# First half of the third pair's values in the visit of its state update, a VectorE read in place of the drain

## Chip, cores, metric

One core of one Trainium2 chip. The time of a run is the device time of the whole program in microseconds. Each engine works through an instruction queue of its own: TensorE (PE, with weight loads as a row of their own, PEld), VectorE (DVE), ScalarE (ACT), GpSimd (POOL) and SyncE (SP), which issues most DMAs.

## What is computed

Block-wise linear attention with decay over 4 batches of 8 heads (768 positions, head size 64), and then, on its output of 3072 tokens by 512, a feed-forward layer with the gate h·cos(h):

```python
for b in range(nb):                       # blocks of 64 positions
    intra = einsum('bhic,bhjc->bhij', qb, kb) * Dmask
    intra = einsum('bhij,bhjd->bhid', intra, vb)
    inter = einsum('bhid,bhde->bhie', qb * lam_pow, kv_state)
    out[:, :, sl] = intra + inter
    kv_state = lam_block * kv_state + einsum('bhsd,bhse->bhde', kb * rev_pow, vb)
# then, with x the attention's output as 3072 x 512
h = x @ w_in                              # 512 x 2048
out = (h * cos(h)) @ w_out                # 2048 x 512
```

## The kernel before

The tokens are cut into 24 blocks of 128, taken in 12 pairs. A pair's two blocks (s = 0, 1) come from two batches. Pairs 0 and 1 (the "spans") are computed in a way of their own at the start. Pairs 2 to 11 run the general code; pair 2 (blocks 4 and 5) is the third pair, and the first of these. The feed-forward layer runs over tiles of blocks (TILES: 4, 2, 2, 2, 2, 2, 2, 4, 4), and pair 2 is the attention for tile 1, done while tile 0's projections run.

A pair's attention on TensorE has these tasks, all of 64-by-64 tiles, four of which fill the array:

- *scores* (L416 to L423): k by q for each half of 64 positions of each block, 32 matmuls into two PSUM banks ps_s; VectorE multiplies by the mask into s_m (L425 to L427).
- *update* (L429 to L435): k by v for the state, 32 matmuls into the banks ps_kv; VectorE adds it to the running sum or writes the state S (L437 to L442), ScalarE casts the sums to S (L444). For pair 2 ("early") VectorE writes the first half's S straight away, and the sums later.
- *values* (L488 to L497): s_m by v, the halves (s=1, half 0) and (s=0, half 1), 16 matmuls into two banks ps_o.
- *values_carried* (L503 to L518): the halves (0, 0) and (1, 1) of the values, 16 matmuls, and then q by S, 32 matmuls (16 where no state is carried in), which add up in the same banks.

The first half of the values writes the banks with other row halves of the array than the second, and has the matmuls that start the accumulation; the second half must not overtake it. The program has three ways for this. Where the next pair's scores and update stand between the halves ("more", pairs 6 to 10), VectorE reads one element of ps_o after the first half ("turn", L499 to L501) and the second half waits for that read. Where the pair is in APART (3, 4, 5, 11), the first half goes to banks of its own, ps_x. For pair 2, which is neither, the queue is drained between the halves (L504, L505).

Nothing is scheduled by hand: a Planner (L56 to L140) gets every task with its engine, a duration, what it depends on, a priority and how many of the eight PSUM banks it takes, and simulates the engines. It takes, at each step, the task that can start first, by priority among equals; a task with `then` set lets only that other task follow on its engine. The order of the planned starts is the order of the instructions in each engine's queue, DMA issues on SP among them. The durations are the program's own estimates (QUART 0.0317 for a group of four small matmuls, SW 0.11 for a change of tile shape), and bear on the order alone.

Around the change the order is: tile 0's projections (L784) in groups of four, three groups for each of four blocks and then each block's last group. The update of pair 2 comes after block 1's last group, values and values_carried together after block 2's, and block 3's last group is held behind values_carried (`closing.deps.append(v12[SPANS])`, L858). Then tile 1's hidden matmuls (L738) begin, which need pair 2's output xT (L520 to L525, copied by VectorE for s = 0 and ScalarE for s = 1). The lines that join scores and update to the plan are L447 to L471; for the early pair the update isn't tied to the scores.

Of the kernel before, what the change touches and what calls it, by code (L numbers as in the profile page):

```python
# [18 lines left out]
SPANS = 2  # L19
# [124 lines left out]
def kernel(  # L144
# [38 lines left out]
    def bank(i, shape, dt, name):  # L183
        return psum.tile(shape, dt, tag=f"bank{i}", bufs=1, name=name)
# [57 lines left out]
    pl = Planner({**BUFS, "q_f": BUFS["ld"], "k_f": BUFS["ld"], "v_f": BUFS["ld"]})  # L242
    MM = lambda cols, n=1: n * (cols / 2400.0 + 0.0025)

    SW = 0.11
# [6 lines left out]
    def prio_attn(n, part):  # L252
        i = next(i for i in range(len(TILES)) if n < first[i + 1])
        return begins[i - 1] + unit[i - 1] * (n - n % 2 - first[i] + 2 * part) / TILES[i]
# [68 lines left out]
    T, So, Vo, d_t, Uo, Uo_sp = ({} for _ in range(6))  # L323
    qkT_head, qk_head, v_head, v12 = {}, {}, {}, {}
    chunks = [(halves[c], c) for c in range(2)]

    def tile_of(n):
        return next((i, n - first[i]) for i in range(len(TILES)) if n < first[i + 1])
# [69 lines left out]
    QUART = 0.0317  # L398
# [71 lines left out]
        qk_head[pr].frees = [T[pr, 0], T[pr, 1], u]  # L470
        return s_t, u  # L471

    def add_stretch(pr):

        n0 = 2 * pr
        g, c = divmod(pr, NB)
        pa = lambda part: prio_attn(n0, part)
        tile_i, j0 = tile_of(n0)

        def value(s, half, o=None):  # L480
            m = halves[half]
            o = live["o", n0 + s][:, :, m] if o is None else o
            for h in range(H):
                yield lambda h=h: nc.tensor.matmul(  # L484
                    o[halves[h % 2], h // 2], lhsT=live["v_s", n0 + s][m, h, :], rhs=live["s_m", n0 + s][m, h, :],
                    start=(apart or s != half) and h < 2, stop=True, skip_group_check=True)

        def values(t):  # L488
            for s in range(2):
                live["o", n0 + s] = bank(t.bank[s], [P, NP, P], F32, "ps_o")  # L490
            cross = [None, None]
            if apart:

                cross = live["cross", pr] = [bank(i, [P, NP, D], F32, "ps_x") for i in t.bank[2:]]
            for x, y in zip(value(1, 0, cross[0]), value(0, 1, cross[1])):
                x()
                y()  # L497

        def turn(_):  # L499

            live["turn", pr] = nc.vector.tensor_copy(spare[D:D + 1, 0:1], live["o", n0][D:D + 1, NP - 1, D:D + 1])  # L501

        def values_carried(_):  # L503
            if not more and not apart:  # L504
                nc.tensor.drain()  # L505
            for x, y in zip(value(0, 0), value(1, 1)):
                i = x()
                y()
                if ("turn", pr) in live:
                    tc.add_manual_dep(i.ins, live.pop(("turn", pr)).ins.name, mybir.DependencyInfo(  # L510
                        mybir.DependencyClass.Sync, mybir.DependencyReason.DATA), reason="row halves in turn")
            for half in range(0 if c else 1, 2):
                S = live["S", pr, 0] if half else live["S", pr - 1, 1]
                for h in range(H):
                    for s, r in enumerate(halves):
                        nc.tensor.matmul(live["o", n0 + s][halves[h % 2], h // 2, halves[half]], lhsT=S[r, h, :],  # L516
                                         rhs=live["qkT", pr][r, 0, h, halves[half]],
                                         start=False, stop=True, skip_group_check=True)  # L518

        def values_out(_, s, e):  # L520
            if ("xT", tile_i) not in live:
                live["xT", tile_i] = work.tile([P, KD, 4 * P], BF16, tag="xT", name="xT")
            j = j0 + s
            (nc.vector.tensor_copy if e == "DVE" else nc.scalar.copy)(  # L524
                live["xT", tile_i][:, :, j * P:(j + 1) * P], live.pop(("o", n0 + s)))  # L525

        def halves_out(_, s, half):
            if ("xT", tile_i) not in live:
                live["xT", tile_i] = work.tile([P, KD, 4 * P], BF16, tag="xT", name="xT")
            o, i = live["o", n0 + s][:, :, halves[half]], (j0 + s) * P + half * D  # L530
            x = live["xT", tile_i][:, :, i:i + D]
            if s == half:
                nc.scalar.copy(x, o)
            elif half or c:
                nc.vector.tensor_add(x, o, live["cross_f", pr][half])  # L535
            else:
                nc.vector.tensor_copy(x, live["cross_f", pr][half])

        def cross_out(_, half):
            live.setdefault(("cross_f", pr), {})[half] = toks.tile([P, NP, D], F32, tag=f"cross{half}", bufs=1, name=f"cross{half}")  # L540
            nc.scalar.copy(live["cross_f", pr][half], live["cross", pr][half])

        deps = [So[n0], So[n0 + 1], Uo[pr, 0], Uo.get((pr - 1, 1)) if c else None]
        more = pr + 1 < NBLK // 2 and pr + 1 not in ALONE
        apart = pr in APART
        v1 = pl.add("PE", 4 * QUART + SW, deps, values, pa(0.5), banks=2 + 2 * apart)
        chain = [v1]
        if more:
            nxt = list(add_scores(pr + 1, pa(0.5)))
            for t in nxt:  # L550
                v1.deps += [d for d in t.deps if d not in nxt]
            chain += nxt
        if more:
            deps = deps + [pl.add("DVE", 0.12, [v1], turn, pa(-9.0))]
        v2 = v12[pr] = pl.add("PE", (12 if c else 8) * QUART + (0.0 if more or apart else 0.28), deps, values_carried, pa(0.5))
        chain.append(v2)
        v1.bank_frees = []
        if apart:
            after = [v2] + ([h_last[tile_i - 2]] if tile_i >= 2 else [])
            copies = [pl.add("ACT", 0.42, after, partial(halves_out, s=s, half=s), pa(0.6)) for s in range(2)]  # L560
            moved = [pl.add("ACT", 0.42, [v1], partial(cross_out, half=half), pa(0.55)) for half in range(2)]
            sums = [pl.add("DVE", 0.4, after + [moved[1 - s]], partial(halves_out, s=s, half=1 - s), pa(0.0 if pr == SPANS else 0.59 - 0.01 * s)) for s in range(2)]
            for s in range(2):
                Vo[n0 + s] = [copies[s], sums[s]]
            v1.bank_frees = [Vo[n0], Vo[n0 + 1], [moved[0]], [moved[1]]]
        for s in range(2):
            So[n0 + s].frees = [v2]
            v_head[n0 + s].frees = [v2]
            if apart:
                continue  # L570
            e = "DVE" if pr == SPANS and s == 0 else "ACT"
            Vo[n0 + s] = [pl.add(e, 0.65, [v2] + ([h_last[tile_i - 2]] if tile_i >= 2 else []), partial(values_out, s=s, e=e),
                                 pa(0.0 if e == "DVE" else 0.6))]
            v1.bank_frees.append(Vo[n0 + s])
        qkT_head[pr].frees = [v2]
        if (pr + 1, 1) in Uo:
            Uo[pr + 1, 1].deps.append(v2)
        for x, y in zip(chain, chain[1:]):
            x.then = y
            y.deps.append(x)  # L580
# [242 lines left out]
    for at, name in enumerate(names):  # L823
        which, n = name[0], int(name[1:])
        soft = which in "io"
        deps = [kept[-3 if soft else -2]] if at and (names[at - 1][0] in "io") != soft else []
        if name == f"q{2 * SPANS}":
            deps = []
        if name == f"v{2 * SPANS}":
            deps = [load_t["k_f", 2 * SPANS]]  # L830
        if name == "o3":
            deps = [load_t["q_f", 2 * SPANS]]
# [10 lines left out]
    add_span_state()  # L843
    for pr in range(SPANS, NBLK // 2):
        prepare(pr)
    add_scores(SPANS, prio_attn(2 * SPANS, 0.2))
    pr = SPANS
    for i in range(len(TILES)):
        while 2 * pr < first[i + 1]:
            if pr + 1 in ALONE:  # L850
                add_scores(pr + 1, prio_attn(2 * pr + 2, 0.2))
            add_stretch(pr)
            pr += 1
        add_ffn(i)
    for f in range(2, SPLIT):
# [60 lines left out]
```

## Time and profile before

| | us |
|---|---|
| median of 4 runs (204.35, 205.24, 204.19, 205.19) | 204.77 |
| the profiled execution, its time | 204.35 |
| its span in the profile | 202.6 |
| PE busy | 194.9 (96%) |
| ACT, DVE, POOL busy | 120.0, 116.6, 64.8 |
| PE hidden L738 and projections L784, busy | 90.5 and 88.3 |

TensorE's granted clock is at 9 tenths or more in every slice (0.999 in the mean). The profile's chain of waits goes back from the last instruction to what released each; a line gives the start, the length and the group of instructions. "issue" is time in which the engine waited for nothing that the profile shows. Other views are groups by source line (shortest, median and longest duration in ns), and the timeline, in which a row merges instructions of one line that follow each other.

VectorE around the change, from the timeline (start, length, group, idle time before it and what ended it):

```profile
42.73 0.77 DVE L352 TENSOR_TENSOR v_s<-v_f,v_scale 128x512 bf16<-128x512 f32 x1 [0.51 <-DMA v_f<-in_v_dram]
44.80 0.69 DVE L440 TENSOR_TENSOR S<-sum,ps_kv 128x512 bf16<-128x512 f32 x1 [1.30 <-PE ps_kv L434]
46.81 0.69 DVE L524 CAST xT<-ps_o 128x512 bf16<-128x512 f32 x1 [1.32 <-PE ps_o L516]
47.42 1.40 DVE L440 TENSOR_TENSOR sum<-sum,ps_kv 128x512 f32<-128x512 f32 x2
```

### The profile page before, as it was taken

The numbers are of one execution on the slowest core, as the hardware profiler recorded it, in microseconds if no ns is written. First come the engines' busy times: TensorE is split into PE (matmuls) and PEld (weight loads), VectorE is DVE, ScalarE is ACT, GpSimd is POOL, SyncE is SP. The second block draws the span as 40 slices with busy tenths as digits, with TensorE's granted clock in tenths as the row PEclk, the third lists the DMA queues.
The fourth block names the chain that finished last, engine by engine and source line by source line (L and its number), as shares of the span: only waits on it lengthen the run. The fifth ranks groups of instructions, "written<-read, shape, count | busy, mean of one in ns | idle before, by whom it ended". The sixth has DMA issues, their size and how long they took to land.

```text
span 202.6 us, 5913 instructions
## 1 busy us (share of the span) xinstructions
PE 194.9 (96%) x2441; PEld 116.9 (58%) x2469; DVE 116.6 (58%) x228; ACT 120.0 (59%) x240; POOL 64.8 (32%) x85
## 2 busy tenths in 40 slices
PE   6999999999999999999999999999999999999994
PEld 2567444547847848666658676755445444444443
DVE  2878774256954967848548575734579544444001
ACT  5978872128937868565639676653877655355120
POOL 5694004056144462726255373543500000000000
PEclk9999999999999999999999999999999999999999
DMA  4999999999999998999899999979900010111112
GB/s 119 320 192 203 204 203 219 176 224 252 211 248 170 282 212 208 227 173 273 166 259 213 212 187 263 203 186 260 209 0 3 3 52 0 52 55 52 52 52 104
DMA packets 96762, 33.94 MB, mean 167 GB/s; under 512 B 84320, under 2 KB 93792, under 8 KB 96736
## 3 DMA queue, kind: packets, MB, share of 16 engines
q1 hardware_dynamic: 89232, 28.78, 64.1%
q0 software_dynamic: 7360, 4.72, 16.2%
q8 instruction: 19, 0.31, 0.6%
q10 hardware_dynamic: 144, 0.07, 0.1%
q14 instruction: 7, 0.06, 0.1%
HBM read 27.27 MB, written 6.29 MB: 166 GB/s over the span
## 4 chain that ended last, share of the span: by engine, by line
PE 92%; DMA 3%; issue 2%; SPq 2%; POOL 1%; ACT 0%; POOLq 0%; ACTq 0%
PE ps_h L738 41%; PE ps_f L784 40%; DMA sp_f<-in_k_dram 3%; PE ps_o L484 2%; PE ps_s L422 2%; PE ps_kv L434 2%; PE ps_o L516 2%; SPq L268 1%; PE ps_o L644 1%; PE ps_kv L631 1%; POOL k_sp L599 1%; PE ps_x L484 0%; PE ps_t L374 0%; PE ps_t L607 0%; PE ps_kv L705 0%
## 5 line engine op out<-in xcount | busy, mean ns | idle before, releaser
L750 DVE TENSOR_TENSOR g<-ps_h,cos 128x256 bf16<-128x256 f32 (+1 forms) x148 | 73.2, 504 | 42.8 <-ACT cos L744 41.9
L744 ACT ACTIVATE cos<-ps_h,halfpi 128x256 f32<-128x256 f32 (+1 forms) x148 | 75.7, 539 | 29.4 <-PE ps_h L738 28.5
L738 PE MATMUL ps_h<-xT,w_in_sb 128*128 128x256 bf16 (+1 forms) x586 | 90.5, 304 | 0.5 <-issue 0.3
L784 PE MATMUL ps_f<-w_out_sb,g 128*128 128x512 bf16 (+2 forms) x378 | 88.3, 370 | 2.0 <-issue 1.3
L738 PEld LDWEIGHTS <-w_in_sb 128*128 128x128 bf16 x592 | 57.1, 98 | 30.2 <-DVE xT L524 0.4
L784 PEld LDWEIGHTS <-g 128*128 128x128 bf16 x400 | 37.6, 98 | 37.2
L344 POOL TENSOR_TENSOR qk<-q_f,q_scale 128x512 bf16<-128x512 f32 x19 | 19.7, 1044 | 38.0 <-DMA q_f<-in_q_dram 29.2
L798 ACT COPY o_sb<-ps_f 128x512 f32<-128x512 f32 (+1 forms) x24 | 13.8, 573 | 30.0 <-PE ps_f L784 29.9
L352 POOL TENSOR_TENSOR v_s<-v_f,v_scale 128x512 bf16<-128x512 f32 x19 | 19.7, 1044 | 15.8 <-DMA v_f<-in_v_dram 13.0
L427 DVE TENSOR_TENSOR s_m<-ps_s,mask 128x512 bf16<-128x512 f32 x20 | 13.0, 685 | 3.6 <-PE ps_s L422 3.0
L348 POOL CAST qk<-k_f 128x512 bf16<-128x512 f32 x18 | 11.0, 613 | 8.0 <-DMA k_f<-in_k_dram 7.8
L524 ACT CAST xT<-ps_o 128x512 bf16<-128x512 f32 x11 | 6.0, 589 | 9.7 <-PE ps_o L516 6.4
L440 DVE TENSOR_TENSOR sum<-sum,ps_kv 128x512 f32<-128x512 f32 x15 | 10.2, 682 | 0.6
L445 ACT CAST S<-sum 128x512 bf16<-128x512 f32 x15 | 9.2, 618 | 0.9 <-DVE sum L440 0.8
L798 DVE COPY o_sb<-ps_f 128x384 f32<-128x384 f32 x1 | 0.6, 558 | 11.5 <-DMA out_dram<-o_sb 11.5
L876 PE MATMUL ps_idle<-blank 128*128 128x512 f32 (+2 forms) x8 | 5.4, 824 | 1.6 <-DVE blank L211 1.6
L484 PEld LDWEIGHTS <-v_s 64*64 64x64 bf16 x320 | 3.9, 107 | 4.1 <-issue 3.6
L623 DVE TENSOR_TENSOR s_m_sp<-ps_s,mask_sp 128x512 bf16<-128x512 f32 x8 | 5.1, 684 | 1.1 <-PE ps_s L618 1.1
L484 PE MATMUL ps_o<-s_m,v_s 64*64 64x64 bf16 x256 | 5.1, 197 | 0.1
L712 POOL CAST S<-sum 128x512 bf16<-128x512 f32 x1 | 0.6, 607 | 14.0 <-DVE sum L709 14.0
L501 DVE COPY spare<-ps_o 1x1 f32<-1x1 f32 x5 | 0.8, 156 | 7.3 <-PE ps_o L484 7.3
L535 DVE TENSOR_TENSOR xT<-ps_o,cross 128x256 bf16<-128x256 f32 x8 | 3.1, 421 | 3.0 <-PE ps_o L516 2.0
(74 smaller groups left out, 96.1 us busy)
## 6 DMA issues: line engine op xcount, KB each, us to landing
q_f<-in_q_dram SPq DMA_DIRECT2D x20, 256.0 KB, 3.7
k_f<-in_k_dram SPq DMA_DIRECT2D x20, 256.0 KB, 4.1
v_f<-in_v_dram SPq DMA_DIRECT2D x20, 256.0 KB, 4.5
out_dram<-o_sb SPq DMA_DIRECT2D x19, 256.0 KB, 2.4
w_out_sb<-in_moe_w_out_dram POOLq DMA_DIRECT2D x4, 512.0 KB, 12.2
sp_f<-in_q_dram SPq DMA_DIRECT2D x2, 512.0 KB, 5.2
sp_f<-in_k_dram SPq DMA_DIRECT2D x2, 512.0 KB, 5.7
w_in_sb<-in_moe_w_in_dram POOLq DMA_DIRECT2D x4, 256.0 KB, 6.9
```

Of the source, the lines that this page charges most:

```text
L344: vec[e].tensor_mul(new_qk()[:, 0, :, s], live.pop(("q_f", 2 * pr + s)), q_scale[:, c, :].unsqueeze(2).to_broadcast([P, H, D]))
L348: (nc.scalar.copy if early else nc.gpsimd.tensor_copy)(new_qk()[:, 1, :, s], live.pop(("k_f", 2 * pr + s)))
L352: vec[e].tensor_mul(live["v_s", 2 * pr + s], live.pop(("v_f", 2 * pr + s)), v_scale[:, c, :].unsqueeze(2).to_broadcast([P, H, D]))
L427: nc.vector.tensor_mul(t, live["s", pr][s], mask.unsqueeze(1).to_broadcast([P, H, D]))
L440: nc.vector.tensor_add(new, live["sum", pr, 0] if half else live["sum", pr - 1, 1], live["kv", pr][half])
L445: nc.scalar.copy(new_S(pr, half), live["sum", pr, half])
L484: yield lambda h=h: nc.tensor.matmul(o[halves[h % 2], h // 2], lhsT=live["v_s", n0 + s][m, h, :], rhs=live["s_m", n0 + s][m, h, :], start= ...
L738: nc.tensor.matmul(t[:, :n], lhsT=w_in_sb[:, kd, f * P:(f + 1) * P], rhs=live["xT", i][:, kd, at], start=(kd == 0), stop=(kd == KD - 1))
L744: nc.scalar.activation(c[:, :n], live["h", i, f, at.start][:, :n], AF.Sin, bias=halfpi)
L750: return nc.vector.tensor_mul(live["g", i][:, f, at], live.pop(("h", i, f, at.start))[:, :n], live.pop(("c", i, f, at.start))[:, :n])
L784: nc.tensor.matmul(live["f", i, j, piece][:, :width], lhsT=live["g", i][:, f, j * P:(j + 1) * P], rhs=w_out_sb[:, f, part], start=(f == 0) ...
L798: (nc.scalar.copy if eng == "ACT" else nc.vector.tensor_copy)(o[:, :width], live["f", i, j, piece][:, :width])
```

## The change

For pair 2 alone, `add_stretch` gets the pair's update task as `ahead`. The task *values* takes over the update's dependencies and priority beside those on s_m, holds its two banks from then on, and is tied to the update, which follows it at once. *values_carried* loses the drain, and waits for the VectorE read "turn" of ps_o, as in the pairs 6 to 10. In the planner's figures for it, the 0.28 of the drain is replaced by one SW.

```diff
-    def add_stretch(pr):
+    def add_stretch(pr, ahead=None):
...
         def values_carried(_):
-            if not more and not apart:
+            if not more and not apart and not ahead:
                 nc.tensor.drain()
...
-        v1 = pl.add("PE", 4 * QUART + SW, deps, values, pa(0.5), banks=2 + 2 * apart)
-        chain = [v1]
+        if ahead:
+            v1 = pl.add("PE", 4 * QUART + SW, [So[n0], So[n0 + 1]] + ahead.deps, values, ahead.prio, banks=2)
+            v1.then = ahead
+            ahead.deps.append(v1)
+            chain = []
+        else:
+            v1 = pl.add("PE", 4 * QUART + SW, deps, values, pa(0.5), banks=2 + 2 * apart)
+            chain = [v1]
...
-        if more:
+        if more or ahead:
             deps = deps + [pl.add("DVE", 0.12, [v1], turn, pa(-9.0))]
-        v2 = v12[pr] = pl.add("PE", (12 if c else 8) * QUART + (0.0 if more or apart else 0.28), deps, values_carried, pa(0.5))
+        v2 = v12[pr] = pl.add("PE", (12 if c else 8) * QUART + (SW if ahead else 0.0), deps, values_carried, pa(0.5))
...
-    add_scores(SPANS, prio_attn(2 * SPANS, 0.2))
+    first_scores, first_update = add_scores(SPANS, prio_attn(2 * SPANS, 0.2))
...
-            add_stretch(pr)
+            add_stretch(pr, first_update if pr == SPANS else None)
```

## The prediction

> **What bounds the kernel now.** I read the page first for what sets the end, then the chain of waits around the change, then the timeline there for what each wait hangs on.
>
> ```profile
> span 202.6 us, 5913 instructions
> PE 194.9 (96%) x2441; PEld 116.9 (58%) x2469; DVE 116.6 (58%) x228; ACT 120.0 (59%) x240; POOL 64.8 (32%) x85
> PE 92%; DMA 3%; issue 2%; SPq 2%; POOL 1%; ACT 0%; POOLq 0%; ACTq 0%
> ```
>
> TensorE carries 92% of the chain that ends last; the other engines are near 60% or below. So the end moves by whatever TensorE's queue gets shorter or longer, as long as nothing new makes it wait. The chain where the third pair (pair 2, blocks 4 and 5) is done:
>
> ```profile
> 40.97 3.40 PE ps_f L784 x15
> 44.37 0.38 PE ps_kv L434 x32
> 44.74 0.54 PE ps_f L784 x2
> 45.28 0.05 issue
> 45.33 0.38 PE ps_f L784
> 45.71 0.25 PE ps_o L484 x16
> 45.96 0.10 issue
> 46.06 0.32 PE ps_o L484 x16
> 46.38 0.28 PE ps_o L516 x32
> 46.66 0.16 issue
> 46.82 0.81 PE ps_f L784 x3
> ```
>
> Columns: start, length, what. The pair comes twice: the update at 44.37, and after one group of four projections (L784) the values at 45.71, both without a break in TensorE's row. Between the two halves of the values stand 0.10 us of nothing, and then a second half of 0.32 us. That is the drain: as an instruction of its own it has a record
>
> ```profile
> L505 PEldq DRAIN  x1: 338/338/338, 45.7 to 45.7; - x1
> ```
>
> (338 ns in the weight loads' queue, partly beside the first half's matmuls). It is the only one in the program: pair 2 alone is neither followed in its visit by the next pair's scores nor among APART.
>
> For what a visit costs without a drain there are two kinds of rows, the APART visit of pair 3 and the visit of pair 6, which waits for the VectorE read instead:
>
> ```profile
> 60.67 0.25 PE ps_x L484 x16
> 60.92 0.13 PE ps_o L484 x16
> 61.05 0.34 PE ps_o L516 x32
> 104.51 0.25 PE ps_o L484 x16
> 104.76 0.26 PE ps_s L422 x32
> 105.02 0.32 PE ps_kv L434 x32
> 105.34 0.16 PE ps_o L484 x16
> ```
>
> The first small group of a visit takes 0.25 us for 16 matmuls, later ones 0.13 to 0.16 for 16 and 0.26 to 0.35 for 32. Whoever comes first in a visit pays about 0.1 us for the change from 128-wide to 64-wide tiles; every visit also ends on 0.16 us of "issue".
>
> **The change, part by part.**
>
> 1. Update visit. It takes 44.74 − 44.37 = 0.37 us. Afterwards the moved half comes first, at 0.25 (the row of any first half), and the 32 update matmuls come behind a group of the same tile shape: 0.29 at 56.82 and 70.15, where they follow scores, 0.32 at 105.02. Sum 0.54 to 0.57, so **+0.17 to +0.20**.
>
> 2. Values visit. It takes 46.82 − 45.71 = 1.11 us with its closing issue. Afterwards: the second half now comes first, 0.25; the 32 carried matmuls 0.28 (here) to 0.35; the issue of 0.16. Sum 0.69 to 0.76, so **−0.35 to −0.42**.
>
> 3. Together **−0.15 to −0.25 us; I take −0.20**. It is nearly the drain alone, for the moved half goes into a visit that is there anyway and pays no tile change of its own. A check the other way: the second half with the drain's gap, 0.10 + 0.32, against 0.16 at 105.34 gives −0.26, the upper end. The Trainium skill ("TensorE: Matmul & The Clock Gate", Single matmul latency) puts a matmul that can't hide its pipe at (398 + N)/2.4 ns when warm, 193 ns for N = 64; the rows' small matmuls are 193 ns each in the middle. A drain would then cost 193 ns less one spacing (0.13/16 = 8 ns), estimated at 0.185 us, and the sum would be −0.185 by the rule against up to −0.26 by the row. I stay with the visits' own rows.
>
> 4. The VectorE read ("turn", L501). Five rows of this form take 156 ns, and start 0.05 to 0.06 us after the first half's end (104.76 to 104.82, 116.88 to 116.93). Here the half ends at about 44.37 + 0.25 = 44.62, so the read stands at 44.68 to 44.84. VectorE's row is empty there: its v_s product ends at 43.50 and the state S starts at 44.80, 0.06 after the update's end. In the new order the update ends at 44.91 to 44.94 and S can't start before 44.97, 0.13 after the read is gone. So the read costs S nothing. If that cover were gone, S would come up to 0.16 later.
>
> 5. The wait for the read. Behind it on TensorE stand the second half, the carried matmuls, block 3's last projections and then tile 1's hidden matmuls; ScalarE's and VectorE's xT copies wait for the carried ones. The visit can't come before the four projections are through, 44.92 + 0.97 = 45.89; the read has been done for 1.05 us by then. Nothing.
>
> 6. S. Before: 44.80 to 45.49, the visit at 45.71, 0.22 of slack. After: 44.98 to 45.67 against 45.89, the same 0.22, and 0.25 more since only the carried matmuls behind the second half read S. Nothing.
>
> 7. The moved half's own waits. It wants both s_m tiles (VectorE, L427, 40.93 + 1.29 = 42.22) and the v_s tiles for which the update waits already (42.95 and 43.50). TensorE gets there at 44.3. Nothing; if the v_s products came 0.9 us later, old and new order would both wait.
>
> 8. PSUM banks. Now 2 banks of ps_o are held from 44.3, beside 2 of ps_kv. The four projections of tile 0 hold 4 at most: blocks 0 and 1 are copied out at 43.54 and 44.40, 2 and 3 at 45.75 and 47.66 (L798). 4 + 4 is exactly 8, and the last of the other four to come free are the scores' banks, at 42.22. It fits with 2 us to spare, but there is no ninth bank.
>
> 9. Semaphores. The Trainium skill ("Perfetto Trace Analysis", Identifying Dependency Chains) warns that an instruction that waits for several engines may get an EventSemaphore instruction put ahead of it, which speaks against joining two tasks with different producers. The trace has such a row at the update of the later visits:
>
> ```profile
> L434 PEldq EVENT_SEMAPHORE  x8: 51/51/51, 56.5 to 152.8; - x8
> ```
>
> Added in both visits at full price, it would take the sum to −0.20 + 2 × 0.05 = −0.10. But the visit at 56.38 has one and its update still takes 0.29: it lies beside matmuls. I count nothing and keep 0.10 for the range.
>
> 10. What it issues and passes: no DMA. Block 2's output copy (45.75) and its store come 0.18 us later, block 3's (47.66) 0.20 earlier; both buffers have time, since the SP queue sends them among loads.
>
> 11. What comes after. From 47.6 on TensorE's row has no wait but the 0.16s and the tile changes; all of it moves up 0.20 us, if the planner keeps its order. Its own figures for the pair shrink by 0.17 (0.28 for the drain goes, 0.11 for a second switch comes), so a visit could slip only where its data are due within 0.17 of the place it has now. In the plan of before, the visits that hang on a DMA have 0.33 us or more; those that hang on S move with the rest. I expect the same order.
>
> Against the profiled execution: 204.35 − 0.20 = 204.15 us, span 202.4. The median of the runs is 204.77, 0.42 above that execution, so **204.57 us**, −0.1%. The four runs lie at 204.19 to 205.24; a difference below 0.5% (1.02 us) is not told from none, and the forecast is "no change" in that sense.
>
> **Rivals.**
>
> *The gain is eaten* (0.10): both event semaphores are paid, or the read does fall in front of S, +0.10 to +0.16, and the moved half costs the upper end. Sum about 0.0, 204.77. For it: the 0.13 between the read's end and S is thin. Against: five rows in which the read lies clear of its neighbours.
>
> *The pair is put off by its banks* (0.16): slower. Place: the update. Two tasks are tied together that need four banks while the four projections hold four. If the planner, with its own times, finds one not free, the tied pair goes behind block 2's projections. Then nothing lies between the update and the carried matmuls: block 3's end waits for the values by the program's own rule, tile 1 for xT. TensorE waits 0.06 + 0.69 (S) + up to 0.16 (the read) + about 0.1 = 0.9 to 1.0 us, less the gain: +0.75. It decides as soon as the scores' banks come free later than block 1's group ends, 2 us from now. If later value visits then slip a group behind too, each loses what the 1.67 us of projections after it (61.55, 74.45, 105.81) no longer cover: the xT copies end at 62.4 and hidden starts at 63.06, so a slip of 0.86 costs 0.2. Two of these: +1.2, 205.97. Against: step 8.
>
> *A better order by luck* (0.10): the shift of 0.17 joins visits downstream or takes tile changes away. A visit's entry (0.1), the wait for the last projection (0.38 against 0.22) and its exit (0.16) are about 0.42; to lose 1.02 in all, two such visits would have to merge: 204.57 − 0.84 = 203.7. Nothing in the profile asks for it. That the change doesn't do what it says is no case of weight: the drain has a single record.
>
> *The forecast* has 0.64.
>
> **Numbers.** Forecast and eaten gain both lie within 0.5%: 0.74 less a little for scatter, 0.72. Slower is the bank rival and scatter, 0.16; faster is the lucky order and scatter, 0.12. Range: bounds of the forecast (−0.25 to 0.0 on 204.77) and the scatter of the runs (about 0.5 either side) give 204.0 to 205.3; a part of each outer case takes it to 203.8 and 205.5.
>
> **What would show it.** No DRAIN record; L501 six times, the first near 44.7; the update visit with 16 ps_o and 32 ps_kv at 0.54 to 0.57; S starting 0.06 after the update, not after the read; the values visit at 0.69 to 0.76; the first hidden matmul of tile 1 0.2 us earlier, and the same distance at the end. Wrong would be: an idle stretch before the update or the carried matmuls, a wait on the read, visits at other places after 50 us.

## The result, and the profile after

| | before | after |
|---|---|---|
| median, us | 204.24 (54 runs) | 203.92 (33 runs) |
| ratio | | 0.9979, 95% interval 0.9973 to 0.9985 |
| the same again, beside later experiments | 204.24 (34 runs) | 203.96 (14 runs), ratio 0.9986 (0.9971 to 1.0001) |
| span of the profiled execution | 202.6 | 202.2 |

The change takes about 0.3 us off: clear of noise in the first interval (that of the later runs just reaches 1), within the half per cent that the forecast called "no change", and somewhat more than the 0.20 that was forecast. The four runs that the prediction had (median 204.77) held two from the thin upper end of this program's runs: 10 of the 54 lie at 204.7 or above. So the forecast of 204.57 was built on a base 0.53 too high; its difference is what to judge. That 203.92 still lies inside the forecast range, 0.12 above its lower end, is owed to the width of the range.

The page after, busy time of TensorE, in which the share of the span is as before:

```profile
span 202.2 us, 5913 instructions
PE 193.8 (96%) x2441; PEld 116.4 (58%) x2469; DVE 116.7 (58%) x229; ACT 120.0 (59%) x240; POOL 64.8 (32%) x85
```

The chain of waits at pair 2 after the change (start, length, what; L485, L517, L745 and L791 are the old L484, L516, L738 and L784):

```profile
44.21 0.25 PE ps_o L485 x16
44.46 0.26 PE ps_kv L434 x32
44.72 0.16 issue
44.88 0.81 PE ps_f L791 x3
45.69 0.25 PE ps_o L485 x16
45.94 0.28 PE ps_o L517 x32
46.22 0.16 issue
46.38 0.81 PE ps_f L791 x3
47.19 7.02 PE ps_h L745 x64
```

The moved half stands ahead of the update; four projections come between, and the second half follows them with no gap. From the first small matmul of the update visit to tile 1's first hidden matmul it was 47.63 − 44.37 = 3.26 us before, and is 47.19 − 44.21 = **2.98: −0.28**. That TensorE also reaches the visit 0.16 earlier in this trace is no effect of the change: the instructions of every engine come in the same order up to there, and the visit begins at 44.20 to 44.31 in all traces below but the last, also in the two that have the order of before (44.27). From hidden to the last copy of the output it is 199.82 − 47.63 = 152.19 before, and 199.36 − 47.19 = 152.17 after (the lines of before, then the last line of after):

```profile
47.63 7.09 PE ps_h L738 x64
199.82 0.27 ACT o_sb L798
199.36 0.27 ACT o_sb L805
```

So the pair is where the time went, and nothing came or went later. That later order has not changed either: of the instruction orders only those at pair 2 differ, and on SP a store of the output that has changed places with one load of q, twice (near 88 and 134 us).

On VectorE, from the timeline:

```profile
44.52 0.16 DVE L502 COPY spare<-ps_o 1x1 f32<-1x1 f32 x1 [1.00 <-PE ps_o L485]
44.80 0.69 DVE L440 TENSOR_TENSOR S<-sum,ps_kv 128x512 bf16<-128x512 f32 x1
45.62 0.21 PEld L485 LDWEIGHTS <-v_s 64*64 64x64 bf16 x16 [0.42 <-DVE S L440]
```

The read is over at 44.68, S begins 0.08 after the update's end. The third row needs care: the weight loads of the second half are said to have waited 0.42 us for S. In the program they wait for the read, not for S, and 0.42 is what most entries into a visit show, nearly all as "issue" (the others 0.21). The chain above has no gap at 45.69. The name in brackets is inferred from the order of events; the eight reads below show that it is not S.

### The profile page after: what moved, and what is told of

The parts are those of the page before. It is cut to its first block, busy times and chain, and to the rows that moved or that the text cites. A ratio compares the mean times of both kernels' runs of the same rounds, so it can differ in the third digit from the quotient of the medians.

```text
span 202.2 us, 5913 instructions
## 1 busy us (share of the span) xinstructions
PE 193.8 (96%) x2441; PEld 116.4 (58%) x2469; DVE 116.7 (58%) x229; ACT 120.0 (59%) x240; POOL 64.8 (32%) x85
## 4 chain that ended last, share of the span: by engine, by line
PE 92%; DMA 3%; issue 2%; SPq 2%; POOL 1%; ACT 0%; POOLq 0%; ACTq 0%
PE ps_h L745 41%; PE ps_f L791 40%; DMA sp_f<-in_k_dram 3%; PE ps_s L422 2%; PE ps_o L485 2%; PE ps_o L517 2%; PE ps_kv L434 2%; SPq L268 1%; PE ps_o L651 1%; PE ps_kv L638 1%; POOL k_sp L606 1%; PE ps_x L485 0%; PE ps_t L374 0%; PE ps_t L614 0%; PE ps_s L625 0%
## 5 line engine op out<-in xcount | busy, mean ns | idle before, releaser
L745 PE MATMUL ps_h<-xT,w_in_sb 128*128 128x256 bf16 (+1 forms) x586 | 90.5, 304 | 0.5 <-issue 0.3
L791 PE MATMUL ps_f<-w_out_sb,g 128*128 128x512 bf16 (+2 forms) x378 | 88.1, 370 | 2.1 <-issue 1.4
L745 PEld LDWEIGHTS <-w_in_sb 128*128 128x128 bf16 x592 | 57.1, 98 | 30.1 <-DVE xT L525 0.4
L791 PEld LDWEIGHTS <-g 128*128 128x128 bf16 x400 | 37.7, 98 | 37.1
L485 PEld LDWEIGHTS <-v_s 64*64 64x64 bf16 x320 | 3.9, 107 | 4.4 <-issue 3.4
L485 PE MATMUL ps_o<-s_m,v_s 64*64 64x64 bf16 x256 | 5.1, 196 | 0.0
```

What stands on the lines that cost most here:

```text
L485: yield lambda h=h: nc.tensor.matmul(o[halves[h % 2], h // 2], lhsT=live["v_s", n0 + s][m, h, :], rhs=live["s_m", n0 + s][m, h, :], start= ...
L745: nc.tensor.matmul(t[:, :n], lhsT=w_in_sb[:, kd, f * P:(f + 1) * P], rhs=live["xT", i][:, kd, at], start=(kd == 0), stop=(kd == KD - 1))
L791: nc.tensor.matmul(live["f", i, j, piece][:, :width], lhsT=live["g", i][:, f, j * P:(j + 1) * P], rhs=w_out_sb[:, f, part], start=(f == 0) ...
```

## Experiments

All times are medians, beside runs of the kernel before with a median of 204.24 in both sets. "Stretch" is the distance used above, from the update visit's start to tile 1's hidden matmuls, in one profiled execution of each kernel; "rest" is from there to the last copy.

| | median | ratio to before (95%) | stretch | rest |
|---|---|---|---|---|
| before | 204.24 | | 3.26 | 152.19 |
| after | 203.92 | 0.9979 (0.9973 to 0.9985) | 2.98 | 152.17 |
| read in place, nothing moved | 204.37 | 1.0001 (0.9991 to 1.0011) | 3.43 | 152.16 |
| moved, drain kept | 204.11 | 0.9999 (0.9986 to 1.0013) | 3.15 | 152.21 |
| after with eight reads | 203.91 | 0.9985 (0.9979 to 0.9991) | 3.03 | 152.09 |
| before with three more drains | 205.10 | 1.0038 (1.0023 to 1.0053) | 4.13 | 152.22 |
| after, late order | 204.18 | 0.9999 (0.9991 to 1.0007) | 2.98 | 152.41 |
| after, two banks more | 204.78 | 1.0022 (1.0013 to 1.0030) | 3.59 | 152.39 |

### The read alone, without the move

The change has two parts, a read for a drain and a move. The first by itself, in the kernel before:

```diff
-            if not more and not apart:
-                nc.tensor.drain()
...
-        if more:
+        if more or pr == SPANS:
             deps = deps + [pl.add("DVE", 0.12, [v1], turn, pa(-9.0))]
-        ... (0.0 if more or apart else 0.28) ...
+        ... (0.0 if more or apart else -0.12) ...
```

(The planner's figure is lowered by what it reckons for the wait, which keeps all other work in the order of before.)

> The kernel before, with the VectorE read between the halves in place of the drain, and nothing moved (all other work in the same order). My theory: the gain lies in the 0.97 us of projections that now stand between the read and its waiter, so a read with nothing to cover it is no cheaper than the drain. 0.06 us to the read, 0.16 for it, 0.06 to 0.1 back, and then a first small group at 0.25 in place of 0.16: 0.37 to 0.41 against the drain's 0.26, so 204.35 to 204.4 us, ratio to before 1.000 to 1.001. Rival (the drain itself is dear and a read is cheap wherever it stands): -0.2 or more, 204.0, ratio 0.999 or less.

Measured: 204.37, in the profile +0.17 of stretch. The chain there:

```profile
45.62 0.28 PE ps_o L484 x16
45.90 0.02 issue
45.92 0.17 DVE spare L501
46.09 0.04 issue
46.13 0.32 PE ps_o L484 x16
```

Between the halves are 0.23 us of waiting for VectorE, and the second half then pays 0.32, as behind a drain. So the read as such is dearer than the drain, and it is free only with the move. (The interval of the ratio includes 1; "dearer" rests on the medians, +0.13, and on the trace.) The theory stands, the rival falls.

### The move alone, with the drain kept

```diff
-            if not more and not apart and not ahead:
+            if not more and not apart:
                 nc.tensor.drain()
...
-        if more or ahead:
+        if more:
             deps = deps + [pl.add("DVE", 0.12, [v1], turn, pa(-9.0))]
```

in the changed kernel; all else keeps its order.

> The changed kernel without the read: the first half stays moved, and the drain stays, now at the head of the values visit, where TensorE changes from 128-wide to 64-wide tiles. Theory A (the drain costs what the array can't take in behind it, and at a change of tiles it has to run empty anyway): 203.9 to 204.05 us, within 0.1 of the change. Theory B (a drain costs 0.2 to 0.26 wherever it stands): 204.1 to 204.2, ratio about 0.9995, and the move alone is worth next to nothing. I lean to something between, 0.1 over the change.

Measured: 204.11, 0.19 above the change; stretch 3.15, +0.17. The visit's head in the chain:

```profile
44.92 0.81 PE ps_f L791 x3
45.73 0.11 issue
45.83 0.32 PE ps_o L485 x16
```

where the change has 0.25 with no gap. Theory B is nearer: also where the tile shape changes, with nothing of the same shape in flight, the drain costs 0.18, two thirds of what it costs between two groups of small matmuls. The move alone is worth 0.11 to 0.13, by the trace and the medians; the interval of the ratio is wide and includes 1, for three of the 22 runs lie at 204.9 to 206.1.

Four stretches now stand side by side. In the old place, the drain has 3.26 and the read 3.43; with the half moved, the drain has 3.15 and the read 2.98. Read for drain costs 0.17 without the move and saves 0.17 with it.

### More reads: how well S is covered

```diff
         def turn(_):
-            live["turn", pr] = nc.vector.tensor_copy(spare[D:D + 1, 0:1], ...)
+            for j in range(8 if ahead else 1):
+                live["turn", pr] = nc.vector.tensor_copy(spare[D:D + 1, j:j + 1], ...)
```

> The changed kernel with eight of the reads in a row on VectorE in place of one; the second half waits for the last. They stand ahead of the state S, which starts at 44.80 in the change. At 0.10 to 0.156 us each they end at 45.3 to 45.77, and S comes 0.5 to 0.97 later. Theory (only the carried matmuls wait for S, so it has 0.22 of slack to the visit and 0.25 more behind the second half): 0.1 to 0.55 us slower than the change, 204.0 to 204.5, and the gap lies between the second half and the carried matmuls. Rival (the whole visit waits for S, as the row of its weight load names it): 0.35 to 0.8 slower, 204.3 to 204.7, with the gap ahead of the second half.

Measured: 203.91, the same as the change, which is less than the theory gave. The reads were shorter than I had put them, 0.66 us for the eight. S began 1.00 us after the start of the update visit (44.27 in this trace), in the change 0.59 after it, so it came 0.41 later:

```profile
44.58 0.66 DVE L503 COPY spare<-ps_o 1x1 f32<-1x1 f32 x8 [1.29 <-PE ps_o L485]
45.27 0.69 DVE L440 TENSOR_TENSOR S<-sum,ps_kv 128x512 bf16<-128x512 f32 x1
```

and in the chain the second half begins on time, while the carried matmuls take 0.33 in place of 0.28:

```profile
45.75 0.25 PE ps_o L485 x16
46.00 0.33 PE ps_o L518 x32
```

A delay of 0.41 that costs 0.05 leaves 0.36 for the slack. The second half doesn't wait for S, which ended at 45.96, 0.21 after that half had begun. Nor do all the carried matmuls: by the program the first 16 read the state of the pair before, and in the trace their weight loads begin by 45.90, those of the other 16 from 46.01 on, 0.05 after S's end. This refutes the rival and what the bracket in the row of the change seems to say.

### More drains: what one costs

```diff
-            for x, y in zip(value(0, 0), value(1, 1)):
+            for j, (x, y) in enumerate(zip(value(0, 0), value(1, 1))):
+                if pr == SPANS and j and j % 2 == 0:
+                    nc.tensor.drain()
```

in the kernel before, so three drains more, one for every four matmuls of the second half.

> The kernel before with three drains more, after each quarter of the second half (each behind four matmuls). If one drain costs the 0.26 us that I read from the two halves' rows, +0.78: 205.0 us, ratio 1.004. Rival (a drain is nearly free, and the gain came from elsewhere): under 0.1 each, 204.5 or less, ratio up to 1.0015.

Measured: 205.10, +0.86; stretch +0.87, so 0.29 for each. Its chain repeats one pattern:

```profile
46.22 0.09 issue
46.31 0.22 PE ps_o L484 x4
46.53 0.09 issue
46.62 0.22 PE ps_o L484 x4
```

0.31 us for four matmuls that take 0.04 otherwise (0.16 for 16). A drain between small matmuls costs 0.27 to 0.29 us, and the change's 0.28 is about the size of one.

### Another order after the pair

```diff
-        ... (SW if ahead else 0.0) ...
+        ... (SW + 0.57 if ahead else 0.0) ...
```

> The changed kernel with the planner's figure for the values visit set 0.57 us longer: nothing changes up to the end of tile 1's hidden matmuls, and from there the planner, which believes TensorE to be later than it is, puts several visits of pairs 3 to 11 one group of matmuls earlier. Theory (the gain lies wholly at pair 2, and the order after it is free as long as no wait appears): 203.8 to 204.1 us. Rival (the order after 50 us matters, so that part of the gain could be luck of the order): visits that come a group of 0.43 to 0.86 us earlier meet states S or transposes that are not ready, 0.2 to 0.3 for each, 204.3 or more; or 0.3 less if it suits them.

Measured: 204.18, 0.26 above the change, with the same stretch of 2.98 and a rest that is 0.24 longer. The theory that the order is free falls; the rival's price was right, though not the wait that it named. The late order loses its time at one place, the visit of pairs 8 and 9:

```profile
127.29 0.06 PE ps_kv L434
127.34 0.02 issue
127.36 0.44 PE ps_kv L434 x31
127.80 0.13 PE ps_o L485 x16
127.93 0.46 PE ps_o L517 x32
```

In the change that visit (at 127.58) takes 0.32 for the update and 0.35 for the carried matmuls; from its first half to its end it is 1.33 us there and 1.60 here. The update stops after one matmul and goes on at 127.36, just after a gate product of VectorE that frees a bank has ended; that it waited for that bank is read from the times alone and wasn't tried. For this study it means: a change of order could have been worth as much as the drain, and the rest of the changed kernel can be compared with that of before because the order is the same.

### Two banks more

```diff
-            v1 = pl.add("PE", ..., values, ahead.prio, banks=2)
+            v1 = pl.add("PE", ..., values, ahead.prio, banks=4)
...
+        if ahead:
+            v1.bank_frees += [[v2], [v2]]
```

> The changed kernel with the moved half holding two banks more until the values visit (unused), so that the moved half and the update together need six of eight banks while the projections hold four. The planner's order up to the values visit is the same; after it, it is the late order with few other differences. The update then needs the bank of block 1, which ScalarE copies out from 44.25 to 44.84 in the change, where the update starts at 44.46. The banks' rival of my prediction in its mildest form: TensorE idles 0.4 to 0.5 us between the moved half and the update, and 204.3 to 204.45 us if the late order is free. If a bank that is short were hidden, 203.9 to 204.1.

Measured: 204.78, 0.86 above the change: 0.61 in the stretch and 0.22 in the rest, close to the late order's 0.24; its order is nearly the late one. From the timeline:

```profile
44.28 0.19 PE L434 MATMUL ps_kv<-v_s,qk 64*64 64x64 bf16 x1
44.87 0.44 PE L434 MATMUL ps_kv<-v_s,qk 64*64 64x64 bf16 x31 [0.40 <-ACT o_sb L807]
```

The update's first matmul runs, the second waits for ScalarE's copy of block 1, and 0.41 us later than in the change the rest begins, at 0.44 in place of 0.26. The wait is the size that I had put; the restart behind it and the order made it 0.86 in all. Had two banks been short, the change would have lost 0.54 us against the kernel before.

### The change again

> The changed kernel as it is. From its trace the pair's two visits give 0.28 us less, from 44.37 to 47.63 before and from 44.21 to 47.19 after. If that is all there is, the median is 203.9 to 203.95 again and the ratio to before 0.9985 to 0.9987. If the ratio of 0.9979 stands, 0.1 to 0.15 us come from elsewhere.

Measured: 203.96, ratio 0.9986 (0.9971 to 1.0001). Eight reads, with 0.05 more of stretch, have 0.9985. So the size is about 0.3 us, what the trace accounts for. The ratio of the medians in the first set is 0.9984 too; that its 0.9979 contains a chance share of the upper end fits the counts (204.7 or more: 10 of 54 runs before and none of 33 after; in this set 4 of 34 and 1 of 14), but wasn't tried. The profile of this run caught one execution of the upper end, at 205.44 us. Its chain:

```profile
35.67 8.94 DMA v_f<-in_v_dram
44.61 0.02 issue
44.63 0.94 DVE v_s L352
45.57 0.04 issue
45.62 0.32 PE ps_o L485 x16
```

The load of block 5's v landed at 44.61, 8.94 us after its issue; in the first trace of the change it took 6.8, and VectorE could start on it at 42.72. TensorE waited 1.26 us for v_s ahead of the moved half. The kernel before needs the same tile at the same place. Whether the other runs of the upper end are of this kind isn't shown: no other was profiled.

## Why the prediction held, and where its size was off

The forecast was no change within 0.5%, −0.20 us, and it was that with the sign right; measured −0.3, in the traces −0.28. By its steps:

- **Steps 1 and 2, the two visits.** The values visit went from 1.11 to 0.25 + 0.28 + 0.16 = 0.69, the lower end of what was given. The update visit went from 0.37 to 0.25 + 0.26 = 0.51, below the range of 0.54 to 0.57: I had taken the 32 update matmuls at 0.29 to 0.32, as they stand behind 32 score matmuls, and they took 0.26, the time of the scores behind a first half (104.76). This term was 0.03 to 0.06 too high. With the middle taken in both steps, it made −0.20 of −0.28, which lies outside the −0.15 to −0.25 of step 3. In step 3 the check from the two halves' rows had −0.26, and a drain in three copies then cost 0.27 to 0.29: here the row of the thing removed was a better guide than the middle of two estimated visits.
- **Step 3, the rule against the row.** By the Trainium skill's figure for a single matmul ("TensorE: Matmul & The Clock Gate", Single matmul latency, given there for the full array) a drain was estimated at 0.185. It costs 0.27 to 0.29 here. In the rows of the three more drains the slow group makes 0.22 − 0.04 = 0.18 of it, near the estimate, and the rest is 0.09 in which TensorE stands still, which the estimate had left out. (The ends of matmuls are modelled in the profile, so it is the sum that is measured, not this division.) The row was right.
- **Steps 4 and 5, the read.** 0.31 us after the visit's start as forecast (44.52 against 44.21), 156 ns, and nothing waited. That it is the four projections that hide it was argued; the read in place, with none between, costs 0.13 to 0.17 more than the drain.
- **Step 6, S.** Slack 0.22 + 0.25 was given; the eight reads put it at about 0.36. The term was too large, with no effect on the sum.
- **Step 7, the moved half's waits.** Right in the usual execution. The case named there, v_s late by more than 0.9 us, is real: one profiled run has it.
- **Step 8, banks.** Right; two more cost 0.61 in the stretch. The form of the rival was not as I had put it: with two banks short the planner left the tied pair in its place, and TensorE waited inside the update, after its first matmul.
- **Step 9, semaphores.** The change's trace has the same eight event-semaphore rows at L434, from 56.0 on, and none at the moved half.
- **Step 11, the order.** Kept, but for the two swaps on SP. The margins in the plan were the reason given, and the late order shows that the order matters: 0.24.
- **The 0.16 of "issue".** The prediction read it as a cost at the end of visits, in step 11 and in the exit of the lucky order. It is the place of a matmul without a record. In the traces of before and after, 2441 matmuls are recorded for 2469 weight loads; the late order's trace has all of them, none of these gaps, and four projections where the others have three:

```profile
PE 196.7 (97%) x2469; PEld 116.4 (57%) x2469; DVE 116.2 (57%) x229; ACT 120.1 (59%) x240; POOL 64.4 (32%) x85
44.82 0.97 PE ps_f L791 x4
```

(The first line is from the page, the second from the chain.) Four projections in the stream take 0.86, so the way back to 128-wide tiles costs about 0.11. The sum isn't touched: the gap is there before and after.

## What to carry to other kernels

Price a drain by the gap and the restart behind it in its own rows, not by the length of its record: 338 ns there were 0.28 us on the path, and 1.2 us at the head of a visit were 0.18. A wait on another engine in place of a drain was worth it here with work put between; where nothing stood between, the wait was the dearer of the two. And where a planner orders the work, hold its order fixed when one part of a change is tried alone, or the order's own price hides the part's.

## Not expected of the hardware

- A drain at a change of tile shape is not free: 0.18 us at the head of the visit, beside the 0.25 that the first group takes there without it. Its record reads 1213 ns, nearly all of it beside the projections ahead of it:

```profile
L506 PEldq DRAIN  x1: 1213/1213/1213, 44.6 to 44.6; - x1
```

- VectorE's smallest reads run into each other: one takes 156 ns, eight in a row 0.66 us, 82 ns each.
- A group of small matmuls that is held up pays its start again: the update's 31 matmuls took 0.44 behind a wait for a bank, the 32 took 0.26 in the stream. Its weight loads were no slower, 30 in 0.33 us there and 32 in 0.35 in the stream; what shows is about the length of one matmul's record, 0.19, which the work ahead covers in the stream.
- A load took 8.94 us from issue to landing in one execution, 6.8 in another of the same program, and TensorE waited 1.26 us for what is made from it.
